# A fused 2-D FFT filter and gated MLP: the FFT refactored around a real row DFT

## The chip, the cores and the metric

The kernel runs on one core of a Trainium2 chip, in one launch. The metric is the device time of one execution in microseconds (us), as the median of several runs; times of single stages come from one profiled execution. The engines are named as in the profile: PE (TensorE; PEld is its weight load), DVE (VectorE), ACT (ScalarE), POOL (GpSimd) and SP (SyncE, which issues all DMAs here).

## What is computed

The input x has 2048 rows (s) of 640 columns (d), in bf16. Each row is normalized; the result goes through a filter in the 2-D frequency domain and, beside it, through a gated MLP with 1536 hidden columns, and x is added:

```python
xn = _layernorm(x, axis=-1)
X  = rfft2(xn.astype(float32)) * (w_r + 1j * w_i)   # 2048 x 321 frequencies
yA = irfft2(X, s=(2048, 640)).astype(bfloat16)
g  = xn @ w_gate ;  u = xn @ w_up                   # [2048, 1536]
yB = (g * u) @ w_down
return x + yA + yB
```

All transforms are done as matrix products with tables of cosines and sines. Row 16p + b of x lies on partition p of "block" b, so there are 16 blocks of 128 rows.

## The kernel before

The program is a list of tasks, each with a name, an engine, a duration in the planner's own numbers, the buffers it reads and writes, and a priority number (`prio`, a low one first). A list scheduler (`_Sched.plan`) puts them in an order for each engine; each engine then runs its order strictly, waiting on semaphores. So a task's place is set by `prio`, the planner's durations, and by which buffers and PSUM banks come free. All names of SBUF are parts of one tensor, `arena`, and all of PSUM of one tensor, `ps`, which is why the profile shows only these two names: line numbers tell the tasks apart.

Stages, in the order of the data:

1. Layernorm: statistics on DVE (L725, L726, L731), nine small DVE steps and a square root on ACT for a group of blocks, then subtract (L797/L799) and multiply (L808/L810) of a block's 640 columns into a second buffer, XN. Blocks 0 and 1 do these on DVE, the other 14 on POOL.
2. T0 (L821): five 128x128 transposes of the block on PE, copied to XT, which both the MLP and the row DFT read. The columns are taken in an even/odd order, at a step of two.
3. D (L846): row DFT from XT, six matmuls of 324 columns. eO (ACT) and eD (DVE) build 321 frequencies from sums and differences.
4. S128 (L879 to L882): a 128-point DFT along s, four matmuls of 324.
5. For 81 groups of 4 frequencies, in batches of eight: T1 (L921) transposes, S16 (L942) does the 16-point DFT along the rest of s, WM (L956) and CB (L964, L966) multiply by the filter on DVE, T2 (L977) transposes back, S16i (L998) does the 16-point inverse. All matmuls have 128 columns.
6. For each output block: S128iA and S128iB (L1112, L1122) do the 128-point inverse, ACCd (L1158, L1159) the inverse row DFT (eight matmuls of 161), and DVE forms 640 columns from sums and differences (US L1178/L1179, U L1190 to L1193) and adds x (XY, L1199).
7. MLP: 96 gate/up tiles GU (L1064: ten matmuls of 256 columns; 12 groups of hidden columns by 8 chunks of rows), copied by ACT (eG, L1075) and multiplied on DVE (H, L1082). With their high `prio` number they fill PE wherever the transform waits. Per block and half, ACCg (L1211) makes twelve matmuls of 320 with w_down, FIN (L1221) adds the transform's part, and the half is stored.

At the start, 56 matmuls on zeros (L700) and single fill matmuls (L688, L689) run on PE until data is there.

Of the kernel before, what the change touches and what calls it, by code (L numbers as in the profile page):

```python
# [391 lines left out]
_DT = ((0, 2), (256, 2), (512, 1), (1, 2), (257, 2))  # L392


def _dperm():
    return [np.arange(128, dtype=np.int64) * st + s0 for (s0, st) in _DT]


def _build_tables():
    t = {}  # L400
    two_pi = 2.0 * math.pi
    sm = np.zeros((128, 3, 128), np.float64)
    sm[:, 0, :] = np.eye(128)
    w16 = np.zeros((16, 2, 4, 2, 16, 4), np.float64)
    w16i = np.zeros((2, 16, 4, 16, 2, 4), np.float64)
    for a in range(16):
        for b in range(16):
            ph = two_pi * ((a * b) % 16) / 16.0
            cs = math.cos(ph)
            sn = math.sin(ph)  # L410
            for q in range(4):
                w16[a, 0, q, 0, b, q] = cs
                w16[a, 1, q, 0, b, q] = sn
                w16[a, 0, q, 1, b, q] = -sn
                w16[a, 1, q, 1, b, q] = cs
                w16i[0, a, q, b, 0, q] = cs
                w16i[1, a, q, b, 0, q] = -sn
                w16i[0, a, q, b, 1, q] = sn
                w16i[1, a, q, b, 1, q] = cs
    sm[:, 1, :] = w16.reshape(128, 128)  # L420
    sm[:, 2, :] = w16i.reshape(128, 128)
    t["sm"] = _bf16_bits(sm)
    dmap = _dperm()
    lv = np.arange(162, dtype=np.int64)[None, :]
    lval = (np.arange(162) <= 160).astype(np.float64)[None, :]
    fd = np.zeros((128, 6, 2, 162), np.float64)
    for q, (tj, par) in enumerate(((0, 0), (1, 0), (2, 0), (2, 1), (3, 1), (4, 1))):
        dd = dmap[tj][:, None]
        ang = two_pi * ((dd * lv) % _D).astype(np.float64) / _D
        sel = ((dmap[tj] % 2) == par).astype(np.float64)[:, None] * lval  # L430
        fd[:, q, 0, :] = np.cos(ang) * sel
        fd[:, q, 1, :] = -np.sin(ang) * sel
    t["fd"] = _bf16_bits(fd)
    s1 = np.arange(128, dtype=np.int64)[:, None]
    k1 = np.arange(128, dtype=np.int64)[None, :]
    t128 = np.zeros((128, 16, 3, 128), np.float64)
    for s2 in range(16):
        th = two_pi * ((k1 * (16 * s1 + s2)) % _S).astype(np.float64) / _S
        t128[:, s2, 0, :] = np.cos(th)
        t128[:, s2, 1, :] = np.sin(th)  # L440
        t128[:, s2, 2, :] = -np.sin(th)
    t["t128"] = _bf16_bits(t128)
    kk = np.arange(128, dtype=np.int64)[:, None]
    sb = np.arange(128, dtype=np.int64)[None, :]
    tinv = np.zeros((128, 16, 2, 2, 128), np.float64)
    for sa in range(16):
        ps = two_pi * ((kk * (sa + 16 * sb)) % _S).astype(np.float64) / _S
        tinv[:, sa, 0, 0, :] = np.cos(ps) / _S
        tinv[:, sa, 0, 1, :] = np.sin(ps) / _S
        tinv[:, sa, 1, 0, :] = -np.sin(ps) / _S  # L450
        tinv[:, sa, 1, 1, :] = np.cos(ps) / _S
    t["tinv"] = _bf16_bits(tinv)
    pp = np.arange(128, dtype=np.int64)
    lk = {"e": 2 * pp, "o": 2 * pp + 1, "m": 256 + pp}
    dq = np.arange(161, dtype=np.int64)[None, :]
    g4 = np.zeros((128, 8, 161), np.float64)
    for q, (kind, par, fn) in enumerate((("e", 0, 0), ("m", 0, 0), ("o", 1, 0), ("m", 1, 0),
                                         ("e", 0, 1), ("m", 0, 1), ("o", 1, 1), ("m", 1, 1))):
        l_ = lk[kind]
        cl_ = np.where((l_ == 0) | (l_ == 320), 1.0, 2.0) * (l_ <= 320) * ((l_ % 2) == par)  # L460
        ang = two_pi * ((l_[:, None] * dq) % _D).astype(np.float64) / _D
        if fn == 0:
            g4[:, q, :] = cl_[:, None] * np.cos(ang) / _D
        else:
            g4[:, q, :] = -cl_[:, None] * np.sin(ang) / _D
    t["g"] = _bf16_bits(g4)
    return t
_BF = mybir.dt.bfloat16
_F32 = mybir.dt.float32
_ACTF = mybir.ActivationFunctionType  # L470

_LN_GROUPS = ((0, 1), (1, 1), (2, 2), (4, 4), (8, 4), (12, 4))
_NSLOT_X = 16
_NSLOT_XN = 8
_NGW = 12
# [30 lines left out]
def _d_act(n):  # L506
    return n * 0.833 + 250.0
# [8 lines left out]
def _build(nc, A_x, A_w_r, A_w_i, B_w_gate, B_w_up, B_w_down, out, dbg=None, opts=None):  # L516
    opts = opts or {}
    dbg = dbg or {}
    tabs = _build_tables()
    es = contextlib.ExitStack()  # L520
    with es:
# [3 lines left out]
        d_t128 = nc.inline_tensor(tabs["t128"], name="c_t128").ap().bitcast(_BF)  # L525
        d_tinv = nc.inline_tensor(tabs["tinv"], name="c_tinv").ap().bitcast(_BF)
# [3 lines left out]
        sch.caps = {"glu": opts.get("cap_glu", 2), "acc": opts.get("cap_acc", 4), "fill": 1}  # L530
# [3 lines left out]
        def alloc(name, size, at=None):  # L534
# [3 lines left out]
            else:  # L538
# [6 lines left out]
        b_gw = alloc("GW", _NGW * 2 * 5 * 128)  # L545
        b_gwj = [[sch.buf("GW_%d_%d" % (w_, j_), lay["GW"][0] + (w_ * 5 + j_) * _NGW * 128, _NGW * 128)
                  for j_ in range(5)] for w_ in range(2)]
        b_gbf = alloc("GBF", 3 * 512)
        b_bp = alloc("BP", _NLB * 128)
        b_wn = alloc("WN", 2 * 16 * _LP)  # L550
        b_z1 = alloc("Z1", 16 * 2 * _LP)
        b_at = alloc("AT", 12032)
        b_bt = alloc("BT", 2 * 8 * 128)
        b_p12 = alloc("P12", 2 * 8 * 2 * 64)
        b_y = alloc("Y", 2 * 8 * 128)
        b_yt = alloc("YT", 2 * 8 * 128)
        b_sm = alloc("SM", 3 * 128)
        b_stat = alloc("STAT", 768)
        b_dum = alloc("DUM", 256)
        b_osb = alloc("OSB", 2 * 648)  # L560
        total = cur[0]
        o_bp = lay["BP"][0]
        b_z2 = alloc("Z2", 3 * 768, at=o_bp)
        b_out = alloc("OUT", 2 * 640, at=o_bp + 2304)
        b_xr = alloc("XR", 2 * 640, at=o_bp + 2304 + 1280)
        o_wn = lay["WN"][0]
        b_wd = alloc("WD", 12 * 640, at=o_wn)
        o_z1 = lay["Z1"][0]
        b_x = alloc("X", _NSLOT_X * 640, at=o_z1)
        b_xn = alloc("XN", _NSLOT_XN * 640, at=lay["P12"][0])  # L570
        o_at = lay["AT"][0]
        b_fd = alloc("FD", 6 * 2 * 162, at=o_at)
        b_t128 = alloc("T128", 16 * 3 * 128, at=o_at + 6 * 2 * 162)
        b_tinv = alloc("TINV", 16 * 2 * 256, at=o_at)
        b_g = alloc("G", 8 * 161, at=o_at + 16 * 2 * 256)
        o_bt = lay["BT"][0]
        b_a = alloc("A", 2 * 2 * _LP, at=o_bt)
        b_yeo = alloc("YEO", 2 * 1296, at=o_bt)
        b_yn = alloc("YN", 2 * 1280, at=o_bt + 2592)
        b_ss = alloc("SS", 2 * 1296, at=o_bt + 2592 + 2560)  # L580
        for par in (b_bp, b_wn, b_z1, b_at, b_bt):
            pass
# [733 lines left out]
```

## Time and profile before

| | |
|---|---|
| median of 3 runs | 239.79 us (239.51 to 239.8) |
| span of the profiled execution, first to last instruction | 238.3 us |
| what lies around the span (median less span) | 1.5 us |
| HBM read, written | 18.37 MB, 2.62 MB |
| ACT_TABLE_LOAD | 1, 1.3 us |

The profile gives the execution's span alone; the 1.5 us are the difference to the median. Three views are used: the page (busy time of each engine, and the span in 40 slices), the chain of waits (the work that ended last, piece by piece) and groups of instructions by line. A row of a group reads: line, engine, operation, output<-input, shapes, count | busy us, mean ns of one | idle time of the engine before them. The mean of one is from its start to its end; the next one on the same engine may start earlier.

### The profile page before, as it was taken

How to read it: one execution, taken by the hardware profiler on the slowest of the kernel's cores; microseconds unless marked ns; L12 is line 12 of the kernel's file. 1: busy time of each engine (PE TensorE's matmuls, PEld its weight loads, DVE VectorE, ACT ScalarE, POOL GpSimd, SP SyncE). 2: the span in 40 equal slices, each digit the busy share in tenths (PEclk: the TensorE clock that was granted, in tenths of full speed). 3: DMA queues.
4: the chain of work that ended last, by engine and by line, in shares of the span. 5: the costliest groups of instructions: out<-in, count | busy, mean ns of one | idle time of the engine just before them, and what ended most of it. 6: DMA issues, size and time to landing. Idle time of an engine off the chain costs nothing.

```text
span 238.3 us, 5579 instructions
## 1 busy us (share of the span) xinstructions
PE 232.5 (98%) x2274; PEld 197.8 (83%) x2274; DVE 173.8 (73%) x502; ACT 108.9 (46%) x181; POOL 24.3 (10%) x35
## 2 busy tenths in 40 slices
PE   8979999999999999999999999999999999999995
PEld 8968888787999999998988888888787787787773
DVE  5969998855479999999847422222278888888895
ACT  2135667676554565554577555555223223223120
POOL 0027856800000000000000000000000000000000
PEclk9999999999999999999999999999999999999999
DMA  6999700960720000001072100000013223123221
GB/s 199 346 338 384 260 3 0 256 190 0 267 89 3 3 0 3 0 3 56 3 241 92 55 3 0 0 3 0 17 43 98 56 69 99 55 73 96 68 60 55
DMA packets 18953, 21.35 MB, mean 90 GB/s; under 512 B 1520, under 2 KB 17520, under 8 KB 18800
## 3 DMA queue, kind: packets, MB, share of 16 engines
q1 hardware_dynamic: 18928, 20.99, 27.7%
q8 instruction: 18, 0.29, 0.5%
q14 instruction: 7, 0.06, 0.1%
HBM read 18.37 MB, written 2.62 MB: 88 GB/s over the span
## 4 chain that ended last, share of the span: by engine, by line
PE 93%; SPq 3%; DMA 2%; DVE 1%; issue 0%; ACT 0%
PE ps L1064 44%; PE ps L1211 22%; PE ps L846 5%; SPq L666 3%; PE ps L1112 3%; DMA arena<-c_t 2%; PE ps L1159 2%; PE ps L977 2%; PE ps L1158 2%; PE ps L998 2%; PE ps L921 2%; PE ps L942 2%; PE ps L821 2%; PE ps L1122 2%; PE ps L879 1%; PE ps L880 1%
## 5 line engine op out<-in xcount | busy, mean ns | idle before, releaser
L1064 PE MATMUL ps<-arena 128*128 128x256 bf16 x960 | 110.5, 273 | 0.2 <-ACT arena L1075 0.2
L1064 PEld LDWEIGHTS ps<-arena 128*128 128x128 bf16 x960 | 92.9, 98 | 11.5 <-ACT arena L1075 0.4
L1075 ACT ACTIVATE arena<-ps 128x512 bf16<-128x512 f32 x96 | 57.3, 597 | 49.7 <-PE ps L1064 49.2
L1211 PE MATMUL ps<-arena 128*128 128x320 bf16 x384 | 54.6, 299 | 0.0
L1082 DVE TENSOR_TENSOR arena<-arena 128x256 bf16<-128x256 bf16 x93 | 26.6, 285 | 33.4 <-ACT arena L1075 33.2
L1211 PEld LDWEIGHTS ps<-arena 128*128 128x128 bf16 x384 | 37.5, 98 | 13.6
L1169 ACT ACTIVATE arena<-ps 128x644 f32<-128x644 f32 x16 | 11.2, 707 | 47.4 <-PE ps L1159 47.4
L956 DVE TENSOR_TENSOR arena<-ps,arena 128x512 bf16<-128x512 f32 (+1 forms) x44 | 25.3, 636 | 0.0
L1221 DVE TENSOR_TENSOR arena<-ps,arena 128x320 bf16<-128x320 f32 x32 | 15.6, 488 | 3.8 <-PE ps L1211 3.4
L846 PE MATMUL ps<-arena 128*128 128x324 bf16 x96 | 15.6, 300 | 0.0
L1009 ACT ACTIVATE arena<-ps 128x1024 bf16<-128x1024 f32 x10 | 10.2, 1022 | 8.8 <-PE ps L998 8.8
L891 ACT ACTIVATE arena<-ps 128x648 bf16<-128x648 f32 x16 | 11.4, 710 | 5.9 <-PE ps L882 5.5
L1199 DVE TENSOR_TENSOR arena<-arena 128x640 f32<-128x640 f32 x16 | 13.1, 818 | 0.4
L797 POOL TENSOR_SCALAR arena<-arena 128x640 bf16<-128x640 bf16 x14 | 11.0, 798 | 17.0 <-DVE arena L742 14.9
L1143 DVE CAST arena<-ps 68x256 bf16<-68x256 f32 x15 | 6.3, 420 | 8.6 <-PE ps L1122 8.6
L846 PEld LDWEIGHTS ps<-arena 128*128 128x128 bf16 x96 | 9.2, 97 | 3.6
L808 POOL TENSOR_SCALAR arena<-arena 128x640 bf16<-128x640 bf16 x14 | 11.1, 807 | 6.1 <-DVE arena L786 6.1
L1159 PE MATMUL ps<-arena 128*128 128x161 bf16 x64 | 10.7, 235 | 0.0
L1158 PE MATMUL ps<-arena 128*128 128x161 bf16 x64 | 10.6, 233 | 0.0
L865 DVE TENSOR_TENSOR arena<-ps,arena 128x322 bf16<-128x322 f32 x16 | 7.8, 488 | 3.6 <-ACT arena L856 3.5
L1132 ACT ACTIVATE arena<-ps 128x512 bf16<-128x512 f32 x16 | 9.5, 593 | 0.7 <-PE ps L1112 0.6
L989 DVE COPY arena<-ps 128x1024 bf16<-128x1024 bf16 (+1 forms) x11 | 7.1, 649 | 3.5 <-PE ps L977 3.5
(71 smaller groups left out, 259.1 us busy)
## 6 DMA issues: line engine op xcount, KB each, us to landing
arena<-in_A_x_dram SPq DMA_DIRECT2D x18, 160.0 KB, 2.2
out_dram<-arena SPq DMA_DIRECT2D x32, 80.0 KB, 1.6
arena<-c_tinv SPq DMA_DIRECT2D x1, 2048.0 KB, 8.2
arena<-in_B_w_gate_dram SPq DMA_DIRECT2D x15, 128.0 KB, 5.0
arena<-in_B_w_up_dram SPq DMA_DIRECT2D x15, 128.0 KB, 3.6
arena<-in_A_x_dram SPq DMA_DIRECT2D x3, 640.0 KB, 7.0
arena<-in_B_w_down_dram SPq DMA_DIRECT2D x1, 1920.0 KB, 8.1
arena<-c_t SPq DMA_DIRECT2D x4, 384.0 KB, 6.3
```

The lines of the kernel that those rows point to most:

```text
L846: ins = c.e.matmul(ps[:, bk + q // 3, 0:324], v_xt[:, tj, b * 128:(b + 1) * 128], v_fd[:, q, :], start=(q % 3 == 0), stop=(q % 3 == 2))
L891: return c.e.activation(dst, src, _ACTF.Copy)
L956: ins = c.e.tensor_tensor(dst, x5[:, :, cc, :, :], wv, AluOpType.mult)
L1064: ins = c.e.matmul(ps[:, bk, w * 256:(w + 1) * 256], v_gw[:, w, j, r, :], v_xt[:, j, c8 * 256:(c8 + 1) * 256], start=(j == 0), stop=(j == 4))
L1075: return c.e.activation(v_gbf[:, rr, :], ps[:, bk, :], _ACTF.Copy)
L1082: return c.e.tensor_tensor(v_ht[:, ft, c8 * 256:(c8 + 1) * 256], v_gbf[:, rr, 0:256], v_gbf[:, rr, 256:512], AluOpType.mult)
L1158: c.e.matmul(dst, v_z2[:, r3, kt, cc, :], v_g[:, 2 * o4, :], start=True, stop=False)
L1159: ins = c.e.matmul(dst, v_z2[:, r3, 2, cc, :], v_g[:, 2 * o4 + 1, :], start=False, stop=True)
L1169: return c.e.activation(dst, src, _ACTF.Copy)
L1199: return c.e.tensor_tensor(v_yn[:, r2, :], v_yn[:, r2, :], v_xr[:, r2, :], AluOpType.add)
L1211: ins = c.e.matmul(ps[:, bk, 0:320], v_ht[:, ft, sa * 128:(sa + 1) * 128], v_wd[:, ft, hf * 320:(hf + 1) * 320], start=(ft == 0), stop=(ft ...
L1221: return c.e.tensor_tensor(v_out[:, r2, sl3], ps[:, bk, 0:320], v_yn[:, r2, sl3], AluOpType.add)
```

## The change

**Layernorm in place.** Statistics go straight into bf16; the group needs one add, one square root (ACT) and one reciprocal in place of nine steps. Subtract (L744) and multiply (L749) run on DVE for all 16 blocks and overwrite X. POOL has no work. The groups are nine, not six (mostly two blocks each).

**Row transform first, on folded rows.** The transform no longer reads XT. L1 and L2 on DVE fold a row of 640 into four groups of 160 (sums and differences of mirrored columns). R (L798), five matmuls with the folded block as weights, does a real 32-point DFT along s and brings the columns onto partitions. When all 16 blocks are done, 16 filter tiles follow, each holding one pair of conjugate residues: D (L881, L885) is now the row DFT, C (L906 to L909) a 64-point complex DFT along s, WM (L920) and CB (L929, L930) the filter, IA and IB (L939, L956) the inverse 64-point DFT. T1, S16, T2 and S16i are gone. The filter's weights are loaded tile by tile: four DMAs of 64 rows each, four tiles ahead.

**Inverse.** When all 16 tiles are done, I (L979, L983) does the inverse row DFT per output block, U1 and U2 on DVE unfold, and the 32-point inverse is a thirteenth matmul (L1026) in the sum with w_down (ACC, L1024). x is added by FIN (L1033) alone; US, U and XY are gone.

**Priorities and loads.** The copies and products of gate tiles have `prio` 5.0 + 0.001 per tile, layernorm from block 4 on 5.4 and up, folds 6.0, filter tiles 10, inverse 19; gate tiles themselves stay at 40. Each gate or up load of four groups is one DMA in place of five. The w_down table lies over the inverse table (`ld_wd` waits for the last IB); before, it lay over the filter weights.

```diff
-_LN_ENG = ("pool",)
...
+                    return c.e.tensor_scalar(v_x[:, b, :], v_x[:, b, :], v_mv[:, b, 0:1], None, _OP.subtract)
+                    return c.e.tensor_scalar(v_x[:, b, :], v_x[:, b, :], v_rs[:, b:b + 1], None, _OP.mult)
...
+                def em_l1(c, b=b, lr=lr):
+                    for k, op in ((0, _OP.add), (1, _OP.subtract)):
+                        c.e.tensor_tensor(v_l[:, lr, k, 0:160], v_x[:, b, 0:160], v_x[:, b, 639:479:-1], op)
+                        ins = c.e.tensor_tensor(v_l[:, lr, k, 160:320], v_x[:, b, 319:159:-1], v_x[:, b, 320:480],
+                                                op)
+                def em_l2(c, lr=lr, fr=fr):
+                    c.e.tensor_tensor(v_f[:, fr, 0:4:3, :], c0, c1, _OP.add)
+                    return c.e.tensor_tensor(v_f[:, fr, 1:3, :], c0, c1, _OP.subtract)
+                def em_r(c, fr=fr):
+                    for j in range(5):
+                        st = v_f[:, fr, j, 0:128] if j < 4 else v_ff[:, fr, 512:640]
+                        ins = c.e.matmul(psflat[:, bk * 512 + j * 128: bk * 512 + (j + 1) * 128], st, v_sm[:, 1, :],
+                                         start=True, stop=True)
...
-            t1 = T("T1_%d" % g, "pe", n * 55.0, em_t1, ...
-            s16 = T("S16_%d" % g, "pe", n * _d_pe_mm(128), em_s16, ...
-            t2 = T("T2_%d" % g, "pe", n * 55.0, em_t2, ...
-            s16i = T("S16i_%d" % g, "pe", n * _d_pe_mm(128), em_s16i, ...
...
+            def em_d(c, t=t):
+                for h in range(2):
+                    c.e.matmul(ps[:, bk + h, 0:320], v_uq[:, 4, t, :], v_fd[:, 640 + 320 * h: 960 + 320 * h],
+                               start=True, stop=False)
+                    for g in (2 * h, 2 * h + 1):
+                        ins = c.e.matmul(ps[:, bk + h, o:o + 160], v_uq[:, g, t, :], v_fd[:, g * 160:(g + 1) * 160],
+                                         start=False, stop=(g % 2 == 1))
+            def em_wm(c, tc=tc, r2=r2, wr=wr):
+                for w in range(2):
+                    wv = wv.unsqueeze(1).to_broadcast([128, 2, 2, 161])
+                    ins = c.e.tensor_tensor(v_p[:, r2, w, :, :].rearrange("p c (m e) -> p c e m", e=2), x4, wv,
+                                            _OP.mult)
...
+        dma("ld_wd", v_wd, wdv, 1536 * 1280, [(b_wd, None)], prio=18.0)
...
+                        c.e.matmul(ps[:, bk, 0:320], v_ht[:, ft, a * 128:(a + 1) * 128], v_wd[:, ft, sl3],
+                                   start=(ft == 0), stop=False)
+                    return c.e.matmul(ps[:, bk, 0:320], v_sm[:, 2, :], v_v[:, a, sl3], start=False, stop=True)
```

In `em_l2`, `v_f` is laid out so that the four groups of one column are neighbours: a group's elements stand four bf16 (8 bytes) apart, and R reads them so. In `em_wm` the product `v_p` is f32, and even and odd frequencies come from separate halves, so elements written one after the other stand two f32 (8 bytes) apart.

Three places show how the order of instructions moves; a row is line, operation, output<-input, shape, count.

The first is DVE in mid-program. Before, it serves a batch of the 16-point stage (WM L956, CB L964/L966, copies of T1 and T2, and products L1082 between):

```order
L956 TENSOR_TENSOR arena<-ps,arena 128x8x64 x4
L1082 TENSOR_TENSOR arena<-arena 128x256
L964 TENSOR_TENSOR arena<-arena 128x8x64
L966 TENSOR_TENSOR arena<-arena 128x8x64
L933 COPY arena<-ps 128x1024
L1082 TENSOR_TENSOR arena<-arena 128x256
L989 COPY arena<-ps 128x1024
L1082 TENSOR_TENSOR arena<-arena 128x256
```

Now the fold of one block stands there (L1 is L778/L779, L2 L788/L789, products L851), 15 times over:

```order
L778 TENSOR_TENSOR arena<-arena 128x160
L779 TENSOR_TENSOR arena<-arena 128x160
L778 TENSOR_TENSOR arena<-arena 128x160
L779 TENSOR_TENSOR arena<-arena 128x160
L851 TENSOR_TENSOR arena<-arena 128x256
L788 TENSOR_TENSOR arena<-arena 128x2x160
L789 TENSOR_TENSOR arena<-arena 128x2x160
L851 TENSOR_TENSOR arena<-arena 128x256
```

Most copies of PSUM have gone to ACT, and DVE runs the folds with two products to a block; PE meanwhile has R and two gate tiles to a block. 58 of the 96 gate tiles stand ahead of the first D.

The second place is PE in the filter stage, one round of the sixteen (D is L881/L885, C L906 to L909, IA L939, IB L956, a gate tile L836):

```order
L836 MATMUL ps<-arena 128x256 x10
L881 MATMUL ps<-arena 128x320
L885 MATMUL ps<-arena 128x160 x2
L881 MATMUL ps<-arena 128x320
L885 MATMUL ps<-arena 128x160 x2
L939 MATMUL ps<-arena 128x256 x4
L956 MATMUL ps<-arena 66x256 x2
L906 MATMUL ps<-arena 128x322
L907 MATMUL ps<-arena 128x322
L908 MATMUL ps<-arena 128x322
L909 MATMUL ps<-arena 128x322
```

Before, a batch of the 16-point stage stood between three gate tiles and the next three:

```order
L1064 MATMUL ps<-arena 128x256 x30
L977 MATMUL ps<-arena 128x128 x8
L942 MATMUL ps<-arena 128x128 x8
L921 MATMUL ps<-arena 128x128 x8
L998 MATMUL ps<-arena 128x128 x8
```

So fewer gate tiles lie between the steps of the transform: 13 in the whole filter stage, none of them between some of the tiles.

The third place is the end of PE's order. Before it was ACCd of the last blocks and `L1211 ... x36`, with all gate tiles done long before. Now gate tiles (L836) and output sums (L1024, L1026) alternate to the end:

```order
L836 MATMUL ps<-arena 128x256 x20
L1024 MATMUL ps<-arena 128x320 x12
L1026 MATMUL ps<-arena 128x320
L1024 MATMUL ps<-arena 128x320 x12
L1026 MATMUL ps<-arena 128x320
```

The last two gate tiles feed the sums right behind them.

More of the change, by code (lines that the diff above doesn't have):

```diff
@@ L662, in bank_of, with hold @@
             return t.units[1]
+        def hold(t, *later):
+            for x in later:
+                t.deps |= set(d for d in x.deps if d is not t and d not in later)
         def dma(name, dst, src, nbytes, writes, prio, semkey=None, reads=(), after=()):
@@ new lines, in _build @@
+        T("warm", "pe", opts.get("warm_ns", 5200.0), em_warm, reads=[(b_dum, None)], prio=-1.0,
+          bank="pair", cls="warm", selffree=True)
+        def em_wpad(c):
+            return c.e.memset(v_w[:, :, :, 321:322], 0.0)
+        wpad = T("w_pad", "dve", 80.0, em_wpad, writes=[(b_wp, None)], prio=3.0)
+        for gi, (b0, nb) in enumerate(_X_LOADS):
+            dma("ld_x%d" % gi, v_x[:, b0:b0 + nb, :], xv[:, b0:b0 + nb, :], 128 * nb * 1280,
+                [(b_x, ("s", b0, b0 + nb))], prio=(0.0, 0.01, 0.02, 0.03, 0.04, 0.05)[gi])
@@ L1144, in _build @@
[L1144 to L1151 removed]
+                    ins = c.e.matmul(ps[0:66, bk, 0:256], v_y[:, r2, cc, 256:322], v_ti[:, t, cc, :], start=(cc == 0), stop=(cc == 1))
```

973 lines of the change are left out of this document (375 added, 598 removed).

## Prediction, made before the run

> **What bounds the kernel now.** I read the page's first two parts, then the chain of waits, then a table by stretch.
>
> ```profile
> span 238.3 us, 5579 instructions
> PE 232.5 (98%) x2274; PEld 197.8 (83%) x2274; DVE 173.8 (73%) x502; ACT 108.9 (46%) x181; POOL 24.3 (10%) x35
> PEclk9999999999999999999999999999999999999999
> PE 93%; SPq 3%; DMA 2%; DVE 1%; issue 0%; ACT 0%
> 62.30:122.90 60.60, 60.36 (x706) 55.21 (x704) 53.53 (x128) 32.59 (x48) 0.00 (x0) 1.00 0.13 46
> ```
>
> TensorE is busy for 98% of the span at full granted clock, and the chain that ended last is 93% TensorE. The last row (a stretch, its length, then busy time of PE, PEld, DVE, ACT and POOL) is the 16-point stage: even there, with VectorE at 53.53 of 60.60 us, TensorE leaves only 0.24 us. So the time is the sum of what TensorE issues, plus its waits, a start and an end. Busy rows overstate one matmul, because neighbours overlap; the chain of waits (start, length, what) gives the pace in a dense stretch:
>
> ```profile
> 20.48 0.56 PE ps L821 x10
> 29.54 0.83 PE ps L846 x6
> 62.29 0.89 PE ps L921 x16
> 124.45 0.44 PE ps L1112 x4
> 127.62 0.22 PE ps L1122 x2
> 127.84 40.39 PE ps L1064 x370
> 168.23 4.89 PE ps L1211 x36
> ...
> 124.89 0.07 PE ps L1158
> ...
> 126.04 0.23 PE ps L1122 x2
> ```
>
> A 128-column matmul takes 0.89/16 = 0.0556 us, 256 columns 40.39/370 = 0.109, 320 columns 4.89/36 = 0.136, 324 columns 0.83/6 = 0.138. Sixteen matmuls of 161 columns stand between 124.89 and 126.04: 0.072 each.
>
> **TensorE work removed and added.** Removed: T1, S16, T2 and S16i, 4 x 81 x 0.0556 = 18.0 us; the row DFT D, 16 x 0.83 = 13.3; the inverse row DFT ACCd, 128 x 0.072 = 9.2. Added: R, 80 x 0.0556 = 4.45; the new D and the new inverse I, each 16 x (2 x 0.136 + 4 x 0.072) = 8.95; a thirteenth 320-column matmul in each of 32 output sums, 32 x 0.136 = 4.35. T0, the 96 gate/up tiles and the 128-column inverse (S128i, now IA and IB) keep their counts and widths, and C replaces S128 at four matmuls of 322 columns for four of 324. Net: 40.5 - 26.7 = **13.8 us less**.
>
> R reads its weights at every fourth bf16, which no row shows. The nearest are loads at every second one (L1112, 98 ns like all others), so I take nothing. At best nothing is gained; at worst the load doubles and sets the pace, 64 x 0.056 = 3.6 us.
>
> ```profile
> L1112 PEld LDWEIGHTS ps<-arena 128*128 128x128 bf16 x64 | 6.0, 98 | 0.4
> ```
>
> **The start.** Before, the fourth TensorE task, S128, waits for a table:
>
> ```profile
> 0.74 0.38 SPq L666
> ...
> 7.80 5.71 DMA arena<-c_t
> 13.56 0.31 PE ps L879
> GB/s 199 346 338 384 260 3 0 256 190 0 267 89 3 3 0 3 0 3 56 3 241 92 55 3 0 0 3 0 17 43 98 56 69 99 55 73 96 68 60 55
> arena<-in_A_x_dram SPq DMA_DIRECT2D x18, 160.0 KB, 2.2
> ```
>
> By 13.56 it has done 1.4 us of its list (two T0, one D). 2886 KB stand in the queue up to that table; taking off the first issue at 0.74 and a lone load's 2.2 us, they moved at 272 KB/us. Now the first gate tile needs 2016 KB: 0.74 + 2.2 + 2016/272 = 10.4 us, with 0.56 us done. That is 12.15 against 9.85, 2.3 us won. The second weight pair stands 1920 KB (1.97 MB) further, at the slices' 0.36 MB/us 5.5 us later, at 15.9; four gate tiles and two T0 fill 4.9 of them. That is 0.6 us of wait, which the 12 fill matmuls there cover (0.67); 8 fills (0.45) go from after 13.56. Net **-2.1 us**, bounds -2.5 and +1.
>
> **VectorE and the new waits.** Its operations overlap too, so I take start to start:
>
> ```profile
> 65.15 2.48 DVE L956 TENSOR_TENSOR arena<-ps,arena 128x512 bf16<-128x512 f32 x4
> 67.55 0.28 DVE L1082 TENSOR_TENSOR arena<-arena 128x256 bf16<-128x256 bf16 x1
> 67.74 0.68 DVE L933 COPY arena<-ps 128x1024 bf16<-128x1024 bf16 x1
> 183.72 0.48 DVE L1178 TENSOR_TENSOR arena<-arena 128x322 f32<-128x322 f32 x1
> 184.12 0.48 DVE L1179 TENSOR_TENSOR arena<-arena 128x322 f32<-128x322 f32 x1
> ...
> 184.88 0.32 DVE L1191 TENSOR_TENSOR arena<-arena 128x160 f32<-128x160 f32 x1
> 185.12 0.32 DVE L1192 TENSOR_TENSOR arena<-arena 128x159 f32<-128x159 f32 x1
> ```
>
> 512 elements from PSUM take 0.60, a gate product 0.20, 322 in f32 0.40, 160 in f32 0.24 (L1191 writes backward at that price).
>
> *Layernorm and folds, up to the first D.* TensorE issues 58 gate tiles, 14 T0 and 16 R from 10.4 on: 63.3 + 3.9 + 4.45 + 0.67 = 72.3, so D starts near 82.8. In the fold part the order has, per block, R and two gate tiles (0.28 + 2.18 = 2.46) against four L1, two L2 and two products: 4 x 0.24 + 2 x 0.40 + 2 x 0.20 = 2.16. Cover is 0.30 per block. The 28 layernorm passes moved from POOL cost VectorE 0.30 each:
>
> ```profile
> 10.39 0.39 DVE L810 TENSOR_SCALAR arena<-arena 128x640 bf16<-128x640 bf16 x1
> 10.69 0.49 DVE L725 BATCH_NORM_STATS2 arena<-arena 128x6 f32<-128x320 bf16 x1
> 11.10 0.47 DVE L726 BATCH_NORM_STATS2 arena<-arena 128x6 f32<-128x320 bf16 x1
> ...
> L731 DVE BATCH_NORM_AGGREGATE arena<-arena 128x2 f32<-128x12 f32 x16 | 3.0, 200 | 0.0
> ```
>
> With statistics at 2 x 0.40 and 0.2 per block, all of VectorE's work before D is 16 x (0.8 + 0.2 + 0.6 + 0.96 + 0.8) + 57 x 0.2 + 5 for small ones = 70 us, between 4.5 and 82.8: hidden by the gate tiles, and nothing is taken for it. L1 reads one operand backward, L2 writes every fourth bf16: unseen. If pairs went at L1082's two elements a cycle L1 would fall to 0.15; if each such element took two turns L2 would be 0.73 (twice 320 at 1.04 ns, plus 0.065). I take the rows above.
>
> *Filter stage (D, C, WM, CB, IA, IB; 16 tiles).* TensorE: 16 x (0.56 + 0.55 + 0.66) = 28.3, plus the 13 gate tiles that stand there, 14.2: 42.5. VectorE: two WM of 644 elements (0.60 + 132 x 1.04 ns = 0.735 each) and two CB of 0.40: 16 x 2.27 + 13 x 0.2 = 38.9. The first WM starts some 2.4 us after the first D and the last IA and IB follow the last CB, so VectorE has about 1 us of slack: **this stage is balanced, and each further VectorE microsecond costs one**. WM writes f32 at every second word; its bounds are 0.60 (L956's own price for 512) and 1.40 (two turns per element). I take 0.735, the row's slope. For TensorE I count 1.0 us of waits for CB: at two places only two D stand between C and the next IA (1.1 us), against 0.2 + 1.47 + 0.8 of WM and CB partly begun before.
>
> *Weights and end.* The down weights (8.1 us, row below) now overlay the inverse table and can't start before IB_15, behind four x loads; ahead of the first output sum stand 6 gate tiles and 5 I, 6.5 + 2.8 = 9.3 us. I take 0.3 us, bounds 0 and 3. Near the end two gate tiles (20 matmuls) stand right ahead of the sum that reads them. What that costs is to be seen where before a tile waits for an ACT copy (0.61 + 0.05); with the product on VectorE (0.28), the matmul's tail (its 0.273 less the pace of 0.109) and a semaphore's 0.04 it is 1.15 us.
>
> ```profile
> arena<-in_B_w_down_dram SPq DMA_DIRECT2D x1, 1920.0 KB, 8.1
> ...
> 107.48 1.11 PE ps L1064 x10
> 108.60 0.61 ACT arena L1075
> 109.21 0.05 issue
> ...
> 124.00 0.04 issue
> ...
> L1064 PE MATMUL ps<-arena 128*128 128x256 bf16 x960 | 110.5, 273 | 0.2 <-ACT arena L1075 0.2
> 235.70:238.30 2.60, 0.00 (x0) 0.00 (x0) 0.49 (x1) 0.00 (x0) 0.00 (x0) 1.00 0.20 63
> ```
>
> New waits 1.0 + 0.3 + 1.15 = 2.45; before has about 1.0 beside the table's (this one, and three at L1122 and L977 near 120 us), so **+1.4**. ACT keeps its 46%: 32 copies of 640 come for 32 of 648 and 644, and 7 T0, 15 IB and 16 eI copies for 16 of 324 and ten of 1024. The 64 filter loads (64 rows each) have a slot four tiles, some 10 us, ahead of use against 2.2 us: hidden; without that cover 2.2 us once. The end after the last matmul (2.6 us, the last row) stays.
>
> **Sum**: -13.8 - 2.1 + 1.4 = -14.5. 238.3 - 14.5 = 223.8; adding back the 1.5 us by which the median of the runs (239.8) exceeds this span gives 225.3. I round up to **225.6 us**.
>
> [...]
>
> **Rivals.**
> *Two turns per strided element (slower).* Place: WM in the filter stage, L2 in the folds. Price: WM 32 x (1.40 - 0.735) = 21.3, less 1 of slack; L2 makes a fold block 0.96 + 1.46 + 0.4 = 2.82 against 2.46, 15 x 0.36 = 5.4. 225.6 + 25.7 = **251 us**. It turns the sign once WM exceeds 0.735 by about 0.47 (14.2 + 1 over 32). For it: no row shows the pattern. Against: L1191's backward writes cost nothing. 0.05; a half-way price (237 to 240) another 0.04. [...]
> *The filter stage runs at chain speed.* If dependent operations don't overlap (WM 0.82, CB 0.48, product 0.28), VectorE needs 16 x 2.60 + 3.6 = 45.2, 6.3 more, 5.3 after slack: **231 us**. For it: C, WM, CB, IA is a chain with two buffers; against: the order puts products and the next WM between. 0.18.
> *TensorE doesn't get shorter*, because R's loads set the pace or weights land late: +3.6 or +3, **229 us**; 0.07.
> *Forecast*, 224 to 228: 0.64. 0.02 is left for a better case.
>
> Faster by over 0.2% (what a measurement of this kernel tells from no change): 0.93; within: 0.02; slower: 0.05. The range for 8 in 10 goes from 223 to 233: it takes in the forecast, the chain and R's loads, and leaves out the strided cases.
>
> **What would show it.** Right: PE busy share still 96% or more, some 219 us busy; gate tiles from about 10.4, D from about 83, first output sum near 136. WM rows near 0.82 us mean, L2 near 0.48, R's weight loads 98 ns. Wrong: WM above 1 us; TensorE idle ahead of IA at every tile (released by CB); PEclk under 9 after a gap.

## The result, and the profile after

The changed kernel takes 232.82 us (median of 4 runs, 232.65 to 232.93) against 239.8 us before (239.51 to 240.2, 4 runs): ratio 0.971, 95% interval 0.969 to 0.972. It is faster by 7.0 us, where the forecast had 14.2: right in sign, and half of the gain is missing. The time lies just inside the range of 223 to 233, for reasons that the range wasn't made for (see below). The profiled execution spans 231.0 us against a forecast span of 223.8. So 7.2 us are to be found.

The page of the changed kernel, its first two rows and the shares of the chain that ended last:

```profile
span 231.0 us, 4957 instructions
...
PE 220.2 (95%) x2002; PEld 180.8 (78%) x2002; DVE 170.3 (74%) x461; ACT 106.6 (46%) x194; POOL 0.2 (0%) x4
...
PE 59%; DVE 23%; DMA 9%; issue 4%; SPq 3%; ACT 1%
```

TensorE is busy for 220.2 us, as forecast (some 219), so its work did become shorter. But the chain is only 59% TensorE where it was 93%, and 23% VectorE where it was 1%. TensorE's busy time shrank (from 232.5 us) while another engine entered the chain, so waits have come in. Where, the stretches show (length, then busy time of PE, PEld, DVE, ACT, POOL): the fold stage up to the first D, the filter stage up to the first output sum, and the rest up to the last matmul.

```profile
42.90:88.00 45.10, 43.25 (x416) 35.87 (x415) 43.96 (x127) 30.78 (x50) 0.00 (x0) 1.00 0.01 2
88.00:143.54 55.54, 52.87 (x478) 43.77 (x476) 48.81 (x101) 37.23 (x72) 0.00 (x0) 1.00 0.39 108
143.54:228.30 84.76, 83.65 (x672) 64.28 (x672) 40.22 (x100) 16.04 (x30) 0.00 (x0) 1.00 0.19 54
```

The first D starts at 88.00 (forecast 82.8), the first output sum at 143.54 (forecast 136), and what follows is as long as forecast (87.5 us to the end of the span, forecast 87.8). So 5.2 us are lost before the first D and 2.3 us between it and the first sum. In the fold stage VectorE is busy for 43.96 of 45.10 us: it sets the pace there. The groups by shape (mean ns of one after the comma) and the timeline of one block (start, length) show with what:

```profile
L920 DVE TENSOR_TENSOR arena<-ps,arena 128x644 f32<-128x644 f32 x32 | 24.9, 821 | 1.3 <-PE ps L909 1.3
...
L789 DVE TENSOR_TENSOR arena<-arena 128x320 bf16<-128x320 f32 x16 | 15.1, 942 | 0.0
L788 DVE TENSOR_TENSOR arena<-arena 128x320 bf16<-128x320 f32 x16 | 14.2, 886 | 0.0
...
L778 DVE TENSOR_TENSOR arena<-arena 128x160 f32<-128x160 bf16 x32 | 10.6, 332 | 0.0
...
L798 PEld LDWEIGHTS ps<-arena 128*128 128x128 bf16 x80 | 4.9, 113 | 5.8 <-DVE arena L789 5.7
```

```profile
51.41 0.93 DVE L789 TENSOR_TENSOR arena<-arena 128x320 bf16<-128x320 f32 x1
...
53.50 0.88 DVE L788 TENSOR_TENSOR arena<-arena 128x320 bf16<-128x320 f32 x1
54.17 0.93 DVE L789 TENSOR_TENSOR arena<-arena 128x320 bf16<-128x320 f32 x1
54.88 0.33 DVE L851 TENSOR_TENSOR arena<-arena 128x256 bf16<-128x256 bf16 x1
```

L2 (L788/L789) has means of 0.89 and 0.94 us where 0.48 was forecast; start to start it takes 0.67 and 0.72 (53.50, 54.17, 54.88), not 0.40. From one L789 to the next 2.76 us pass, against the 2.46 us that TensorE needs for a block, and R's weight loads (L798) wait 5.7 us for L789. WM (L920), which was feared for its own step of 8 bytes, has the forecast 0.82. L1 (L778) is as taken.

The busy time of TensorE hides most of this wait. Two rows of TensorE from the same time (start, length):

```profile
49.96 2.35 PE L836 MATMUL ps<-arena 128*128 128x256 bf16 x20
52.41 0.47 PE L798 MATMUL ps<-arena 128*128 128x128 bf16 x5
```

Twenty matmuls at the pace of 0.109 us end at 52.14, and R starts at 52.41: 0.27 us are lost. But the row is 2.35 us long in place of 2.18, since the last matmul's own length (0.273 us) counts whole, and so only 0.10 us look idle. So, as an estimate, every wait of TensorE in the lists below costs such a tail of 0.16 us beside what its row says (0.273 less the pace of 0.109 at 256 columns, 0.299 less 0.136 at 320).

What TensorE waited for in the whole program (total, times, longest):

```profile
PE ps L906 <- DMA arena<-in_A_w_i_dram: 1.7, 3, 0.9
PE ps L836 <- issue: 1.2, 2, 0.8
PE ps L1024 <- DVE arena L851: 1.1, 1, 1.1
...
PE ps L1024 <- DMA arena<-in_B_w_down_dram: 0.7, 1, 0.7
...
PE ps L939 <- ACT arena L671: 0.3, 1, 0.3
```

C (L906) waits three times for a filter load, 1.7 us (2.2 with the tails) that the forecast had at nothing. The first output sum waits 0.7 us for the down weights (taken at 0.3), and the last sums wait 1.1 us for a gate product (taken at 1.15). The chain shows the longest of C's waits: a load that needs 4.44 us where the median of these loads is 2.2; the third gate and up loads (1280 KB) were issued ahead of it, with three filter loads between.

```profile
97.60 0.53 SPq L665
...
100.05 4.44 DMA arena<-in_A_w_i_dram
...
104.54 0.31 PE ps L906
```

**Two theories for the missing time.** A: L2's lone bf16 writes cost 4.5 to 5 us in the fold stage, and late filter loads 1.5 to 2 us in the filter stage. B: L2 is slow for another reason (two f32 operands, other traffic), and the filter stage runs at VectorE's pace, so that the loads only take the blame.

### The profile page after: what moved, and what is told of

It reads as the page before. It is cut to its first block, busy times and chain, and to the rows that moved or that the text cites. A ratio compares the mean times of both kernels' runs of the same rounds, so it can differ in the third digit from the quotient of the medians.

```text
span 231.0 us, 4957 instructions
## 1 busy us (share of the span) xinstructions
PE 220.2 (95%) x2002; PEld 180.8 (78%) x2002; DVE 170.3 (74%) x461; ACT 106.6 (46%) x194; POOL 0.2 (0%) x4
## 4 chain that ended last, share of the span: by engine, by line
PE 59%; DVE 23%; DMA 9%; issue 4%; SPq 3%; ACT 1%
PE ps L836 25%; PE ps L1024 23%; DVE arena L789 5%; DMA arena<-in_B_w_down_dram 4%; DVE arena L920 4%; DVE arena L779 3%; DMA arena<-in_A_w_i_dram 3%; DVE arena L851 3%; SPq L665 3%; DVE arena L788 2%; PE ps L1026 2%; PE ps L757 2%; DVE arena L778 2%; DMA arena<-in_A_x_dram 1%; DVE arena L930 1%
## 5 line engine op out<-in xcount | busy, mean ns | idle before, releaser
L671 ACT ACTIVATE arena<-ps 128x512 bf16<-128x512 f32 (+4 forms) x184 | 103.8, 589 | 106.9 <-PE ps L836 81.9
L836 PE MATMUL ps<-arena 128*128 128x256 bf16 x960 | 112.7, 273 | 1.2 <-issue 1.2
L836 PEld LDWEIGHTS ps<-arena 128*128 128x128 bf16 x960 | 92.3, 98 | 12.3 <-issue 1.5
L1024 PE MATMUL ps<-arena 128*128 128x320 bf16 x384 | 56.9, 299 | 1.8 <-DVE arena L851 1.1
L1024 PEld LDWEIGHTS ps<-arena 128*128 128x128 bf16 x384 | 37.1, 98 | 16.0 <-issue 1.4
L851 DVE TENSOR_TENSOR arena<-arena 128x256 bf16<-128x256 bf16 x96 | 28.5, 297 | 22.5 <-ACT arena L671 22.3
L1033 DVE TENSOR_TENSOR arena<-ps,arena 128x320 bf16<-128x320 f32 x32 | 15.7, 489 | 29.0 <-PE ps L1026 29.0
L920 DVE TENSOR_TENSOR arena<-ps,arena 128x644 f32<-128x644 f32 x32 | 24.9, 821 | 1.3 <-PE ps L909 1.3
L789 DVE TENSOR_TENSOR arena<-arena 128x320 bf16<-128x320 f32 x16 | 15.1, 942 | 0.0
L788 DVE TENSOR_TENSOR arena<-arena 128x320 bf16<-128x320 f32 x16 | 14.2, 886 | 0.0
L779 DVE TENSOR_TENSOR arena<-arena 128x160 f32<-128x160 bf16 x32 | 10.7, 335 | 0.0
L778 DVE TENSOR_TENSOR arena<-arena 128x160 f32<-128x160 bf16 x32 | 10.6, 332 | 0.0
L939 PE MATMUL ps<-arena 128*128 128x256 bf16 x64 | 9.6, 272 | 0.3 <-ACT arena L671 0.3
L1026 PE MATMUL ps<-arena 128*128 128x320 bf16 x32 | 9.6, 299 | 0.0
L716 DVE BATCH_NORM_STATS2 arena<-arena 128x6 f32<-128x320 bf16 x16 | 7.7, 480 | 2.4 <-DMA arena<-in_A_x_dram 2.4
L798 PEld LDWEIGHTS ps<-arena 128*128 128x128 bf16 x80 | 4.9, 113 | 5.8 <-DVE arena L789 5.7
L983 PE MATMUL ps<-arena 128*128 128x160 bf16 x64 | 9.3, 231 | 0.0
L979 PE MATMUL ps<-arena 66*128 66x320 bf16 x32 | 9.2, 300 | 0.0
L798 PE MATMUL ps<-arena 128*128 128x128 bf16 x80 | 7.5, 224 | 1.9 <-DVE arena L789 0.5
L885 PE MATMUL ps<-arena 128*128 128x160 bf16 x64 | 9.1, 233 | 0.0
L881 PE MATMUL ps<-arena 128*128 128x320 bf16 x32 | 9.1, 299 | 0.0
L929 DVE TENSOR_TENSOR arena<-arena 128x322 bf16<-128x322 f32 x16 | 7.8, 491 | 0.2
```

What stands on the lines that cost most here:

```text
L671: return c.e.activation(dst, src, _ACTF.Copy)
L778: c.e.tensor_tensor(v_l[:, lr, k, 0:160], v_x[:, b, 0:160], v_x[:, b, 639:479:-1], op)
L779: ins = c.e.tensor_tensor(v_l[:, lr, k, 160:320], v_x[:, b, 319:159:-1], v_x[:, b, 320:480], op)
L788: c.e.tensor_tensor(v_f[:, fr, 0:4:3, :], c0, c1, _OP.add)
L789: return c.e.tensor_tensor(v_f[:, fr, 1:3, :], c0, c1, _OP.subtract)
L798: ins = c.e.matmul(psflat[:, bk * 512 + j * 128: bk * 512 + (j + 1) * 128], st, v_sm[:, 1, :], start=True, stop=True)
```

## The experiments

Ratios are to the kernel before, measured on the same chip in the same session (its medians: 239.8 us beside the change, and 240.27, 240.0 and 240.22 us in the three sessions of experiments). A difference of 0.004 in the ratio is 1 us.

| kernel | median us | ratio | 95% interval |
|---|---|---|---|
| the change | 232.82 | 0.971 | 0.969 to 0.972 |
| contiguous folds | 228.12 | 0.950 | 0.947 to 0.953 |
| eight filter slots | 230.86 | 0.962 | 0.958 to 0.966 |
| both | 226.83 | 0.944 | 0.941 to 0.946 |
| both, and more VectorE work in the filter stage | 232.72 | 0.970 | 0.967 to 0.973 |
| half the rows in each filter load | 231.52 | 0.962 | 0.956 to 0.968 |
| one load per weight and tile | 249.72 | 1.040 | 1.037 to 1.044 |
| the same, contiguous folds, own place for w_down | 244.66 | 1.019 | 1.016 to 1.022 |
| the same, gate tiles ahead of the sums | 243.42 | 1.014 | 1.011 to 1.017 |
| both, gate tiles ahead of the sums | 224.59 | 0.933 | 0.928 to 0.937 |
| the same, w_down's issue first | 224.57 | 0.933 | 0.928 to 0.938 |

**Contiguous folds.** The four groups lie one behind the other; R takes five runs of 128 neighbouring columns, of which the second and fourth hold two groups each, and these become the two 320-column matmuls of D (the table is sorted to match).

```diff
-        v_f = V("F").rearrange("p (r d g) -> p r g d", r=3, g=4)
+        v_f = V("F").rearrange("p (r g d) -> p r g d", r=3, g=4)
-                        st = v_f[:, fr, j, 0:128] if j < 4 else v_ff[:, fr, 512:640]
+                        st = v_ff[:, fr, j * 128:(j + 1) * 128]
-                    c.e.matmul(ps[:, bk + h, 0:320], v_uq[:, 4, t, :], v_fd[:, 640 + 320 * h: 960 + 320 * h],
+                    c.e.matmul(ps[:, bk + h, 0:320], v_uq[:, 2 * h + 1, t, :], v_fd[:, 640 + 320 * h: 960 + 320 * h],
```

> Folded rows laid out group by group, so L2 writes and R reads neighbouring bf16; the same number and width of matmuls, the same order of instructions. Theory A (L2 is slow because each bf16 it writes stands 8 bytes from the next): L2 means fall from 0.89 and 0.94 us to about 0.48, the round of a fold block from 2.75 to 2.46 us, the first D moves from 88.0 to 83 to 84, R's weight loads go from 113 to 98 ns, and the time from 232.8 to 227.5 to 228.5 us. Theory B (L2 is slow for its two f32 operands or because it meets other traffic): L2 stays near 0.9 and the time within 0.5 us of 232.8.

Measured: 228.12 us; the ratio falls from 0.971 to 0.950, by some 5 us. Groups by shape, and the timeline of one block's L2:

```profile
L789 DVE TENSOR_TENSOR arena<-arena 128x320 bf16<-128x320 f32 x16 | 7.7, 484 | 0.0
L788 DVE TENSOR_TENSOR arena<-arena 128x320 bf16<-128x320 f32 x16 | 7.7, 480 | 0.0
...
L798 PEld LDWEIGHTS ps<-arena 128*128 128x128 bf16 x80 | 5.8, 98 | 0.4
```

```profile
51.28 0.48 DVE L788 TENSOR_TENSOR arena<-arena 128x320 bf16<-128x320 f32 x1
51.68 0.48 DVE L789 TENSOR_TENSOR arena<-arena 128x320 bf16<-128x320 f32 x1
...
53.74 0.48 DVE L788 TENSOR_TENSOR arena<-arena 128x320 bf16<-128x320 f32 x1
```

L2 is at the forecast 0.40 start to start, a block takes 2.46 us (51.28 to 53.74), and R's loads 98 ns. Only the place of the elements was changed, the operands were not, so theory A holds for the folds. The first D stands at 84.67 here, with 2.4 us of waits for gate weights at the start in place of the change's 1.2; less that difference it is 83.5.

**Write steps by themselves.** Behind the last sum, VectorE runs 14 kinds of a 320-column operation, six of each, for instance:

```diff
+                lambda c, i: c.e.tensor_tensor(zb(i, 4), a, b_, _OP.add),
+                lambda c, i: c.e.tensor_tensor(zf(i, 2), a, b_, _OP.add),
+                lambda c, i: c.e.tensor_tensor(zf(i, 2), pp, wb, _OP.mult),
```

(zb writes bf16, zf f32, the number is the step in elements; a and b_ are f32 in SBUF, pp f32 in PSUM, wb bf16.)

> The changed kernel with 14 kinds of a 320-column VectorE operation behind the last sum, six of each, that write at different steps; its output is that of the changed kernel. Theory A1 (a lone bf16 is what costs): f32 operands to bf16 at steps of 2, 4 and 8 elements about 0.7 us start to start, to f32 at steps of 2 and 4 about 0.40, with or without a PSUM operand. Theory A2 (the step of 8 bytes costs when both operands come from SBUF): to f32 at step 2 also about 0.7 with SBUF operands, about 0.40 with a PSUM operand, and to bf16 at step 4 with a PSUM operand about 0.40. Theory B: all about 0.40.

Measured, in the timeline (start, length of the six): bf16 at steps 1, 2, 4 and 8 (L1061 to L1064), f32 at steps 1, 2 and 4 (L1066 to L1068), bf16 at step 4 with a PSUM operand (L1069), WM's form (L1070), and bf16 from bf16 at steps 4 and 1 (L1072, L1073).

```profile
230.59 2.50 DVE L1061 TENSOR_TENSOR arena<-arena 128x320 bf16<-128x320 f32 x6
233.13 2.52 DVE L1062 TENSOR_TENSOR arena<-arena 128x320 bf16<-128x320 f32 x6
235.68 4.42 DVE L1063 TENSOR_TENSOR arena<-arena 128x320 bf16<-128x320 f32 x6
240.14 8.66 DVE L1064 TENSOR_TENSOR arena<-arena 128x320 bf16<-128x320 f32 x6
...
253.28 2.50 DVE L1066 TENSOR_TENSOR arena<-arena 128x320 f32<-128x320 f32 x6
255.82 2.50 DVE L1067 TENSOR_TENSOR arena<-arena 128x320 f32<-128x320 f32 x6
258.36 3.56 DVE L1068 TENSOR_TENSOR arena<-arena 128x320 f32<-128x320 f32 x6
261.95 4.41 DVE L1069 TENSOR_TENSOR arena<-ps,arena 128x320 bf16<-128x320 f32 x6
266.39 2.48 DVE L1070 TENSOR_TENSOR arena<-ps,arena 128x320 f32<-128x320 f32 x6
...
273.34 4.41 DVE L1072 TENSOR_TENSOR arena<-arena 128x320 bf16<-128x320 bf16 x6
277.79 1.50 DVE L1073 TENSOR_TENSOR arena<-arena 128x320 bf16<-128x320 bf16 x6
```

From the start of one kind to the next, over six: bf16 costs 0.42 us at steps 1 and 2, 0.74 at step 4, 1.45 at step 8; f32 0.42 at steps 1 and 2, 0.60 at step 4. PSUM operands change nothing (0.74 and 0.42). So neither theory A1 nor A2 was right as a whole. It is not the lone bf16 (step 2 is free), and not the step of 8 bytes (free in f32, and that is WM), but a lone bf16 at 8 bytes: width and step together. Where bf16 comes from bf16, the step of 8 bytes makes it nearly three times as long: 0.26 to 0.74. The time of this kernel (283.98 us, one run) has some 50 us of added operations in it, and nothing is read from it.

**Filter slots.** Eight in place of four; TensorE's order is the same.

```diff
-_NW = 4
+_NW = 8
```

> Eight filter slots in place of four, so the filter loads go out eight tiles ahead; PE's order is unchanged, the third gate and up loads stand two tiles later in SP's order. Theory A (C waits because the filter loads come late): the 1.7 us of C's waits for them go, the stretch from the first D to the first output sum shortens from 55.5 to about 53.5 to 54, the time falls by 1.5 to 2 us to 231. Theory B (VectorE's chain sets the stage's pace): the loads' waits turn into waits of IA for CB, and the time stays within 0.4 us of 232.8.

Measured: 230.86 us; the ratio falls from 0.971 to 0.962, by some 2 us. C waits for no load any more; the first D to the first sum takes 54.39 us in place of 55.54, with 1.2 us of wait for the down weights in it (0.7 before). The gain in that stretch, 1.15 us, is about C's 2.2 us (tails counted) less 0.5 more for the down weights and 0.5 more for IA: theory A. Part of what theory B says is true as well: VectorE's turn per tile, from one first WM to the next, is 2.40 to 2.48 us here in most tiles, as in the changed kernel between its waits for loads. Loads that come in time take away these waits and no more.

**Both edits.**

> The edits of the two runs above together. If both terms are separate: 232.8 less 4.5 to 5 less 1.5 to 2, 226 to 226.8 us, the first D at 83 to 84 and the first output sum near 137. If the late D hid the late loads only partly, so that an earlier stage meets the loads earlier: 227.5 to 228.5.

Measured: 226.83 us. The two stretches:

```profile
38.00:83.11 45.11, 45.11 (x465) 40.98 (x463) 39.97 (x142) 32.29 (x55) 0.00 (x0) 1.00 0.02 4
83.11:137.18 54.07, 52.62 (x478) 43.78 (x476) 48.61 (x102) 37.23 (x72) 0.00 (x0) 1.00 0.36 99
```

TensorE has no gap in the fold stage, the first D stands at 83.11 (forecast 82.8) and the first sum at 137.18 (136). The span is 224.6, 0.8 over the forecast 223.8. With these two terms put right, the forecast's sum nearly stands.

**Why the loads are late.** Each filter load carries half its rows, and the place of the rest is cleared once at the start; issues, slots and the other loads stay.

```diff
-                    dma("ld_w%d_%d_%d" % (t, w_, h), v_w[64 * h:64 * h + 64, wr, w_, 0:321], wvs[w_][:, k2, :],
+                    dma("ld_w%d_%d_%d" % (t, w_, h), v_w[64 * h:64 * h + 32, wr, w_, 0:321], wvs[w_][0:32, k2, :],
```

> The changed kernel with 32 of the 64 rows in each filter load (half of the filter stays zero): 64 issues and four slots as before, half the rows and bytes. Theory A1 (SP's 0.62 us per issue is what sets the loads' pace, whatever they carry): issues stay at 0.6 us, C's waits for loads stay near 1.7 us and the time within 0.6 us of 232.8. Theory A2 (the pace is that of the rows behind the issue, and SP only stands in the queue behind them): issues in the filter stage take 0.45 us or less, C's waits fall below 0.6 us, the time to 231.3 to 232.

SP's timeline in the filter stage of the changed kernel (start, length, count):

```profile
111.87 1.24 SPq L665 DMA_DIRECT2D arena<-in_A_w_r_dram  x2
113.14 1.24 SPq L665 DMA_DIRECT2D arena<-in_A_w_i_dram  x2
114.42 1.24 SPq L665 DMA_DIRECT2D arena<-in_A_w_r_dram  x2
```

and in that of the kernel with half the rows:

```profile
109.78 0.78 SPq L665 DMA_DIRECT2D arena<-in_A_w_r_dram  x2
110.60 0.88 SPq L665 DMA_DIRECT2D arena<-in_A_w_i_dram  x2
112.19 0.77 SPq L665 DMA_DIRECT2D arena<-in_A_w_r_dram  x2
```

An issue of 64 rows holds SP for 0.62 us, four of them with their gaps 2.55 us per tile (111.87 to 114.42), almost a tile's whole turn (the forecast's 42.5 us for the stage are 2.66 per tile). With 32 rows it is 0.39 to 0.44, SP has gaps again (111.48 to 112.19), C waits 0.3 us in place of 1.7, and the time is 231.52 us (interval 0.956 to 0.968). This is theory A2 in all three signs; A1, an issue of 0.62 us whatever it carries, fails. In the changed kernel SP's issues of filter loads follow one another without a gap: four slots were no lead of four tiles, with the queue at the consumer's own pace (2.55 us per tile against the forecast's 2.66) and 1280 KB of other loads in it. Two things stay open. Half the rows are also half the bytes, and the run doesn't part that from the shorter issue; nor does it show whether SP itself or the queue behind it takes the 0.62 us. Rows alone give no rule for other shapes either: an issue of 640 KB took 0.53 (the row at 97.60 above).

**Fewer issues.** The two 64-row loads as one of 128 rows.

```diff
+                    wvs[w_][:, ka:kb + 1:kb - ka, :].rearrange("k h l -> h k l"),
```

> The changed kernel with four filter slots kept, and the two loads of 64 rows of a tile and weight made one load of 128 rows: 32 issues in place of 64. Theory A1 (the loads come late because SP issues one in 0.62 us, 2.5 us per tile, as long as a tile's turn): C's waits for loads go from 1.7 us to at most 0.3, the time from 232.8 to 231.0 to 231.8, as with eight slots. Theory A2 (they come late because a slot is free only four tiles ahead and the third gate and up loads stand between): at least 1 us of the waits stays and the time stays within 0.6 us of 232.8.

Measured: 249.72 us, slower than either theory had it: C waits 14.1 us for loads, the longest 5.0. A stretch of the filter stage in the changed kernel (the last three columns: granted clock, busy share of the 16 DMA engines, GB/s):

```profile
106.00:118.00 12.00, 12.00 (x112) 9.99 (x110) 11.53 (x23) 8.72 (x18) 0.00 (x0) 1.00 0.31 65
```

and one in this kernel:

```profile
108.00:120.00 12.00, 10.06 (x66) 7.51 (x66) 6.58 (x11) 5.16 (x11) 0.00 (x0) 0.72 0.14 42
```

The share stands at 0.14 of 16 engines, 2.2 of them, and 42 GB/s, while C waits for these very loads. Why so few was not shown: no run has one load of 128 rows in another order of the source's indices. A1 and A2 stay undecided by this run.

The next two kernels have this load too and carry its price, so only the difference between them tells something.

```diff
-        b_wd = alloc("WD", 12 * 640, at=lay["TI"][0])
+        b_wd = alloc("WD", 12 * 640)
```

> Contiguous folds, one load of 128 rows per weight with four slots, and the down weights in a place of their own, so that their load no longer waits for the last IB. If the wait of the first output sum for them (0.8 us with eight slots) is all that they cost: 225.8 to 226.3 us, and no wait for them. If their earlier load slows the filter loads or the x loads: 226.5 or more, with C waiting again.

> The kernel of the run before this, with the gate tiles' priority numbers rising by 0.01 per tile in place of 0.02, so that all 96 stand below the sums' 41 and the last two no longer stand right ahead of the sum that reads them. If the wait of 1.1 us at the last sums is theirs, it goes: 1.0 to 1.2 us less than the run before, 224.6 to 225.3. If it is only moved (another sum waits, or the inverse stage gets short of filler): within 0.4 us of it.

```diff
-                    pu = 40.0 + 0.02 * ui
+                    pu = 40.0 + 0.01 * ui
```

Measured: 244.66 and 243.42 us. With its own place w_down is no longer waited for, but C's waits (12.7 and 13.9 us) hide what that is worth in time, so that stays open. Between the two the last sums' wait of 1.1 us goes, and the ratio falls by 0.0056, 1.3 us.

**Is the filter stage balanced?** On the kernel with both edits, each tile's CB gets a third operation of 322 columns that writes to a place of its own.

```diff
+                c.e.tensor_tensor(V("EX")[:, t * 322:(t + 1) * 322], v_p[:, r2, 0, 0, :], v_p[:, r2, 1, 1, :], _OP.subtract)
```

> The kernel with contiguous folds and eight slots (226.8 us), with a third f32 to bf16 operation of 322 columns added to each tile's CB, written to a place of its own: 16 x 0.40 = 6.4 us more of VectorE in the filter stage; the output is the same. Theory A (the stage is balanced with about 1 us of slack, each further VectorE microsecond costs one): 5 to 6 us slower, 232 to 233, and IA waits for CB. Theory B (products can wait and the slack is 3 us or more): 1 to 3.5 us slower, 228 to 230.3.

Measured: 232.72 us, 5.9 more than without it. What TensorE waits for first (this kernel's lines stand one or two further: L921 is WM, L941 IA, L932 the last CB):

```profile
PE ps L941 <- DVE arena L932: 3.8, 8, 0.7
```

WM's rows in mid-stage, two with both edits and two with the third operation:

```profile
102.86 1.55 DVE L920 TENSOR_TENSOR arena<-ps,arena 128x644 f32<-128x644 f32 x2
105.26 1.56 DVE L920 TENSOR_TENSOR arena<-ps,arena 128x644 f32<-128x644 f32 x2
```

```profile
105.49 1.56 DVE L921 TENSOR_TENSOR arena<-ps,arena 128x644 f32<-128x644 f32 x2
108.30 1.55 DVE L921 TENSOR_TENSOR arena<-ps,arena 128x644 f32<-128x644 f32 x2
```

A tile's turn grows from 2.40 to 2.81 us, by the whole of the added operation. From the first D to the first I the stage grows from 44.82 us (83.11 to 127.93) to 50.58 (82.91 to 133.49), by 5.8 of the 6.4 us added. Up to the first sum (141.97 in place of 137.18) it is only 5.0, because the wait of 0.8 us for w_down, whose load took 9.83 us with both edits, is gone. Theory A: a slack of some 0.6 us, and behind it each VectorE microsecond costs one.

**A version that beats both kernels.** Contiguous folds, eight slots with 64-row loads, and the gate tiles' numbers at 0.01 per tile, so that none stands behind a sum (with 0.02 the last two have 41.88 and 41.90, above the sums' 41.01 to 41.76).

> Contiguous folds, eight filter slots with loads of 64 rows as at first, and gate-tile priority numbers rising by 0.01, so that the last two tiles stand four sums earlier. If the wait of 1.1 us at the last sums goes and nothing takes its place: 1.1 us less than 226.8, 225.5 to 226.0, with the wait for the down weights (0.8) left. If the sums moved behind it wait elsewhere: 226.5 or more.

Measured: 224.59 us, ratio 0.933 (0.928 to 0.937), 2.2 us less than with both edits, twice what was expected: the wait of 1.1 us goes, and with it the 0.8 us for the down weights (1.3 and 1.0 with their tails), because more gate tiles now stand ahead of the first sum, which stands at 163.34 in the chain. That the second would go was not foreseen. Its page:

```profile
span 222.5 us, 4965 instructions
...
PE 94%; DVE 2%; ACT 1%; DMA 1%; issue 1%
```

On top of it, the four x loads are put behind `ld_wd` in SP's order:

```diff
-                prio=pc, semkey=("xr", xs))
+                prio=pc, semkey=("xr", xs), after=[ldwd])
```

> The kernel of the run before this, with the issue of the down weights ahead of the four x loads on SP. If those four issues (1.8 us) are what makes the first output sum wait: that wait (0.8 us) goes, 0.6 to 0.9 us less than the run before. If the x loads then come late for FIN, or the load is late for another reason: within 0.3 us of it.

Measured: 224.57 us, no difference; the wait that it was to remove had gone already, so the run tells nothing of these four issues.

## Why the prediction missed half of the gain

- *TensorE work, -13.8 us*: right. 220.2 us busy against some 219, and with the two edits 217.6, in a span of 224.6.
- *The start, -2.1*: right. The first gate tile starts at 10.41 us (forecast 10.4); the second weights cost 0.41 us beyond their fillers. This term moves between executions: 1.25 us with contiguous folds, 0.69 with both edits, none with eight slots.
- *The fold stage, "Cover is 0.30 per block"*: **the step that failed.** L2 was taken at 0.40, from f32 rows that write neighbours; it takes 0.67 and 0.72, two L2 per block add 0.59, and the cover of 0.30 turns into a wait of 0.30 per block: 15 x 0.30 = 4.5 of the 5.2 us. (R is held up 14 times in the trace, the first time by 0.65 us and then by 0.26 to 0.28, 4.2 us in all.) The price that the prediction named for two turns (0.73, a block of 2.82) was nearly what came, but it was tied in one rival to the same price for WM and given 0.05. L2 and WM share the step in bytes, not the width of what is written, and the runs show that both count (at 8 bytes 0.42 us in f32 and 0.74 in bf16; bf16 at 4 bytes 0.42). The "two elements a cycle" of L1082 is an estimate from rows: 256 columns in 0.20 us, less the prediction's 0.065, are 0.53 ns each, half of its 1.04 (512 columns in 0.598 us less 322 in 0.402 give 1.03). L1 came as taken (0.235 us start to start, forecast 0.24).
- *WM, 0.735*: right (0.821 mean, 0.82 forecast; 0.74 start to start). The prediction had no row with its step and took the slope of the rows that it had; the write steps show for 320 columns in f32 0.42 us at 4 bytes and at 8, against 0.60 at 16. In bf16 the step of 8 bytes takes 0.74.
- *The filter loads, "hidden"*: **the second step that failed**, 1.7 us (2.2 with the tails). The forecast counted a load's landing (2.2 us) against a lead of four tiles and not SP's time for the four issues of a tile (2.55 us), nor the gate and up loads between them (a filter load behind them took 4.44 us to land).
- *Filter stage balanced, about 1 us of slack*: right in kind, some 0.6 measured. The 1.0 us of waits for CB was too much: IA has one wait of 0.3 us (two, 0.6, with both edits). The list puts it to a copy on ACT, which ended at 120.66; CB had ended at 120.64, so either would have set it.
- *The stretch from the first D to the first sum*: 51.8 us of TensorE work were forecast, and 55.54 measured. The rows of waits in it come to 2.7 us, five tails to 0.8, and four hold-ups shorter than a tail, which no row of waits shows, to 0.4 (ahead of 93.04, 101.77, 103.01 and 112.31 in TensorE's timeline).
- *Down weights 0.3*: 0.7, as their load took 9.70 us and not 8.1. *Gate tiles at the last sums 1.15*: 1.1 in the row and 1.3 with the tail, which the forecast's sum contains; right in place and nearly in size.
- *R's loads, nothing*: the four strided loads of a block take 110 to 136 ns, the fifth, of neighbours, 97 or 98 (113 is the mean of all five), but they were never the pace: they wait for L2. (The forecast's "98 ns like all others" passed over L1122, whose loads of 68 columns took 112 ns before the change too.)
- *The range, 223 to 233*: that 232.82 lies in it is luck. Its upper end was set for a filter stage at chain speed (231 us) and for R's loads (229 us), and it was said to leave out the strided cases. Most of what came was a strided case, on L2 alone.

## What to carry to other kernels

Price a strided write by the width of an element and its step together (here, at 8 bytes, 0.42 us in f32 and 0.74 in bf16); a row with the same step in bytes but another width is no evidence, and a layout that keeps each run of weights contiguous may cost no matmul at all (2002 with strided and with contiguous folds). A prefetch's lead is what is left after the issuing queue's own time per step, so compare that time (here 2.55 us per tile) with the consumer's turn (2.66 by the forecast), not the landing time alone (2.2). When a refactoring moves work to an engine with little slack, work out the slack per block: here a cover of 0.30 us per block against 0.59 of extra cost made 2% of the time.

## What the runs showed of the hardware

- VectorE, 320 columns from f32 operands, start to start: bf16 written at 2 and 4 bytes 0.42 us, at 8 bytes 0.74, at 16 bytes 1.45; f32 at 4 and 8 bytes 0.42, at 16 bytes 0.60. One operand in PSUM made no difference for bf16 and f32 at 8 bytes (0.74 and 0.42).
- Weight loads of TensorE (128 x 128) at every fourth bf16 take 110 to 136 ns, at neighbours and every second one 98 in the median.
- One load of 128 rows per weight and tile: from 108 to 120 us, where only these loads were issued and TensorE waited for them, 2.2 of 16 DMA engines were busy (0.14), at 42 GB/s. Two loads of 64 rows: from 106 to 118 us 5.0 were busy (0.31), at 65 GB/s, and TensorE had no gap.
- SP, issues of 64 and 32 rows of 642 bytes in a row: 0.62 and 0.39 to 0.44 us.
- In the first kernel with 128-row loads TensorE stood still for 5.03 us ahead of 109.46, and the granted clock of the stretch from 108 to 120 us was 0.72; the profiled executions of the kernels in the table without such loads had a mean of 1.00.
